# Remainder rows of k and v as tiles of their own, on all 128 partitions

## The chip, the cores and the metric

The kernel runs on one core of one Trainium2 chip, as one launch. The metric is the device time of the launch in microseconds, as the median of several executions. The core has five engines that run side by side and wait for each other by semaphores: TensorE (matrix products), VectorE, ScalarE, GpSimd and SyncE. Sixteen DMA engines move data between the memory in DRAM (HBM) and the core's own memory, SBUF, which has 128 partitions. In the profile the engines are PE (PEld for its weight loads), DVE, ACT, POOL and SP.

## The reference

Two blocks follow each other, all in float32, for 8 batches, 8 heads of 64, and 576 positions. The first is linear attention: for each head a 64 x 64 matrix from k and v, then q by it, then a root-mean-square norm over the 64. The second is an MLP mixer over the positions ("token") and over the 512 channels.

```python
kv = np.einsum('bhsd,bhse->bhde', k, v)
out = np.einsum('bhsd,bhde->bhse', q, kv)
rms = np.sqrt(np.mean(out * out, axis=-1, keepdims=True) + 1e-06)
x = out / rms * g_norm                       # then (B, H, S, D) -> (B, S, H*D)
...
h = np.maximum(x.transpose(0, 2, 1) @ w_tok1, 0.0) @ w_tok2
u = x + h.transpose(0, 2, 1)
return u + np.maximum(u @ w_ch1, 0.0) @ w_ch2
```

The kernel gets k and v as 8 x 576 x 512 (heads beside each other in the last dimension), q transposed as 8 x 512 x 576, and the weights as 64-bit words that it turns into float32 itself ("decoding").

## The kernel before

The change touches the first stage, attention with the token mixing behind it, which fills the first 186 us or so. Batches are taken in four pairs; `side` is the batch within its pair.

The sum over 576 positions doesn't divide by 128: there are four chunks of 128 positions (`J` = 4, `LO` = 512) and a remainder of 64 (`HF` = 64). `k_in[b % 2]` and `v_in[b % 2]` are tiles of 128 partitions x 5 chunks x 512 (`JJ` = 5). `load(b)`, lines 140 to 147, fills each with two DMAs: the main rows (1 MB), and behind it the 64 remainder rows (128 KB) into partitions 0 to 63 of the fifth chunk. Partitions 64 to 127 of that chunk are set to zero once, by the four memsets on GpSimd at line 1285, so that `kv` can treat it as a full chunk. All of these DMAs go through SyncE's queue, v of batch 0 alone through ScalarE's.

`kv(side, half)`, line 371, makes four of the eight 64 x 64 matrices. For each of two pairs of heads `i` and each chunk `j` it issues two products, one for each head `h`, which take one half of the array's columns each:

```python
matmul(o[ds(h * D, D), i, ds(h * D if whole else 0, D)], lhsT=kk[:, j, at],
       rhs=vv[:, j, at],
       start=(j == 0), stop=(j == JJ - 1), skip_group_check=True)
```

Each product is two passes in the trace, so a batch has 80 passes on `ps_kv`. `evict(side, half)` copies the result to SBUF (`kvp`), on VectorE for batch 0 and on ScalarE for the others. `attend` multiplies q by it; `load_q` (main, 1 MB per batch, tile `qT`) and `load_q_rest` (128 KB, `qR`) bring q. The first pair (`whole`) uses full 128 x 128 products with zeros off the diagonal, the later pairs quarters of the array (64 x 64).

The order of all this is written out by hand in lists of short names, `start`, `middle` and `steady` (lines 1297 to 1319), which `play` walks through; every engine keeps that order. `kv01` is the product of side 0, half 1; `e01` its eviction; `l0` the load of the batch that takes side 0 of the next pair; `a`, `g`, `q`, `t` are parts of the attention, `h` and `u` the two products of the token mixing, `f` a fetch of a block of channel weights and the bare numbers decoding steps. Ahead of the lists come the loads of batches 0 and 1 with two blocks of token weights between them, and the third block, `get_tok1_rem` (line 219), which brings the 64 remainder rows of `w_tok1` twice, into the lower and the upper 64 partitions, by two DMAs.

The DMAs issued by SyncE and ScalarE share eight semaphores in rotation. Each issue waits until the DMA eight issues before it has landed, and besides for the tile that it overwrites.

## Time and profile before

| what | us |
|---|---|
| median of 3 runs | 773.67 (773.21 to 774.2) |
| the profiled execution | 772.69 |
| its span, first instruction to last | 770.6 |
| TensorE busy in the span | 760.8 |
| VectorE, ScalarE, GpSimd busy | 642.8, 277.5, 112.3 |
| passes of k by v (`ps_kv`), from the first to the end of the last | 9.2 to 135.7 |

The page gives for each engine the busy time, its share of the span and the number of instructions, and then the span in 40 slices of 19.3 us with the busy share in tenths. The row of DMA is the mean busy share of the sixteen DMA engines. Matrix products are pipelined, so that a full row of PE says that products follow each other without holes, not that each is as fast as it can be. In a line of a timeline the columns are the start, the length, the engine, the source line, the operation, written tile, read tiles, shape, and the number of instructions; an arrow in brackets tells how long the engine was idle before it and who ended that.

### The profile page before, as it was taken

Reading aid. Unit: us, or ns where it says so; the run is one execution under the profiler, and the core shown is the slowest. Engines: PE = TensorE matmul, PEld = TensorE weight load, DVE = VectorE, ACT = ScalarE, POOL = GpSimd, SP = SyncE. Lnnn points to the kernel's source line nnn. Section 1 sums busy time; section 2 is a strip of 40 time slices with the busy share of each in tenths; the row PEclk is TensorE's granted clock in tenths of the full one; section 3 lists DMA queues with packets and bytes.
Section 4 is the critical chain, followed back from the end, with each engine's and each line's share of the span. In section 5 each row is a group of like instructions: output and inputs, shape, how many; then the busy total and the mean of one; then the engine's idle time right before and its main releaser. Section 6 shows DMA issues by size and latency. Waiting matters only on the chain.

```text
span 770.6 us, 12663 instructions
## 1 busy us (share of the span) xinstructions
PE 760.8 (99%) x4682; PEld 612.8 (80%) x4682; DVE 642.8 (83%) x945; ACT 277.5 (36%) x555; POOL 112.3 (15%) x124
## 2 busy tenths in 40 slices
PE   7999999999999999999999999999999999999998
PEld 6665555445888888888888888888888888888887
DVE  2877897997766779999979889987998996798996
ACT  2466575764210233521144242223352224325221
POOL 1002020113410000002240001042000218000204
PEclk9999999999999999999999999999999999999999
DMA  9999999599799786589898577999659879955679
GB/s 308 318 336 385 378 355 358 187 318 338 251 275 355 261 288 194 163 271 203 221 230 257 152 227 220 251 188 271 196 153 284 175 220 205 209 146 155 152 200 119
DMA packets 137819, 188.29 MB, mean 244 GB/s; under 512 B 48800, under 2 KB 95392, under 8 KB 135712
## 3 DMA queue, kind: packets, MB, share of 16 engines
q1 hardware_dynamic: 101744, 167.54, 68.9%
q0 software_dynamic: 34816, 18.36, 15.9%
q10 hardware_dynamic: 1200, 1.61, 0.6%
q8 instruction: 37, 0.61, 0.3%
q14 instruction: 22, 0.18, 0.1%
HBM read 138.31 MB, written 49.15 MB: 243 GB/s over the span
## 4 chain that ended last, share of the span: by engine, by line
PE 97%; DMA 2%; DVE 1%; SPq 0%; issue 0%; ACT 0%
PE ps_d L135 28%; PE ps_b L135 19%; PE ps_a L135 19%; PE ps_h L135 8%; PE ps_u L135 8%; PE ps_v L135 5%; PE ps_c L135 3%; PE ps_o L135 2%; PE ps_kv L135 2%; PE ps_w L135 2%; DMA qT<-in_q_dram 2%; PE ps_r L135 0%; SPq L123 0%; DVE x L451 0%; DVE ms L472 0%; DVE x L509 0%
## 5 line engine op out<-in xcount | busy, mean ns | idle before, releaser
L135 PE MATMUL ps_d<-ui,w 128*128 128x256 f32 x504 | 118.6, 379 | 0.0
L135 PEld LDWEIGHTS ps_d<-ui,w 128*128 128x128 f32 x504 | 95.8, 190 | 13.0
L132 ACT COPY ps_d<-ps_a 128x768 f32<-128x768 f32 (+1 forms) x56 | 32.0, 571 | 199.9 <-PE ps_a L135 196.8
L126 DVE TENSOR_TENSOR v<-v,v 128x1536 f32<-128x1536 f32 (+2 forms) x70 | 103.3, 1483 | 0.3
L135 PE MATMUL ps_b<-sv,w 128*128 128x256 f32 x324 | 78.9, 379 | 0.0
L135 PE MATMUL ps_a<-v,w 128*128 128x256 f32 x324 | 78.7, 379 | 0.0
L1205 POOL DMA_DIRECT2D out_dram<-us x24 | 26.8, 1832 | 291.8 <-ACT p L132 286.2
L135 PEld LDWEIGHTS ps_b<-sv,w 128*128 128x128 f32 x324 | 61.2, 190 | 8.9 <-issue 0.6
L135 PEld LDWEIGHTS ps_a<-v,w 128*128 128x128 f32 x324 | 61.6, 190 | 8.4
L135 PE MATMUL ps_u<-h,w_tok 128*128 128x512 f32 (+1 forms) x160 | 64.7, 599 | 0.0
L135 PE MATMUL ps_d<-v,w 128*128 128x256 f32 x258 | 62.7, 379 | 0.0
L129 ACT ACTIVATE v<-v 128x768 f32<-128x768 f32 (+1 forms) x54 | 42.7, 822 | 55.1 <-DVE v L126 53.5
L135 PE MATMUL ps_h<-x,w_tok 128*128 128x512 f32 x128 | 57.7, 600 | 0.3 <-DVE w_tok L188 0.3
L1205 POOL DMA_DIRECT2D out_dram<-r x40 | 41.3, 1925 | 102.0 <-ACT p L132 80.2
L135 PE MATMUL ps_d<-sv,w 128*128 128x256 f32 x228 | 55.4, 379 | 0.0
L135 PEld LDWEIGHTS ps_d<-v,w 128*128 128x128 f32 x258 | 48.9, 190 | 6.6
L135 PEld LDWEIGHTS ps_u<-h,w_tok 128*128 128x128 f32 (+1 forms) x160 | 25.6, 179 | 31.1 <-issue 26.7
L135 PEld LDWEIGHTS ps_d<-sv,w 128*128 128x128 f32 x228 | 43.3, 190 | 5.9
L135 PE MATMUL ps_a<-uT,w 128*128 128x256 f32 x192 | 46.7, 379 | 0.0
L135 PEld LDWEIGHTS ps_h<-x,w_tok 128*128 128x128 f32 x128 | 23.4, 190 | 27.2 <-issue 24.3
L135 PE MATMUL ps_b<-ui,w 128*128 128x256 f32 x168 | 40.8, 379 | 0.0
L135 PEld LDWEIGHTS ps_a<-uT,w 128*128 128x128 f32 x192 | 36.5, 190 | 5.0
(165 smaller groups left out, 1291.4 us busy)
## 6 DMA issues: line engine op xcount, KB each, us to landing
w<-parts SPq DMA_DIRECT2D x168, 384.0 KB, 3.8
w<-parts SPq DMA_DIRECT2D x56, 192.0 KB, 3.8
uT<-blocks SPq DMA_DIRECT2D x36, 256.0 KB, 5.6
k_in<-in_k_dram SPq DMA_DIRECT2D x8, 1024.0 KB, 13.3
qT<-in_q_dram SPq DMA_DIRECT2D x8, 1024.0 KB, 12.7
out_dram<-x POOLq DMA_DIRECT2D x16, 512.0 KB, 7.5
v_in<-in_v_dram SPq DMA_DIRECT2D x7, 1024.0 KB, 15.8
raw<-in_moe_w_ch_dram SPq DMA_DIRECT2D x8, 768.0 KB, 12.4
```

The costliest lines, as they stand in the source:

```text
L126: keep(engine.tensor_tensor(out=o, in0=a, in1=b, op=op))
L129: keep(nc.scalar.activation(o, a, AF.Relu))
L132: keep(nc.scalar.copy(o, a))
L135: keep(nc.tensor.matmul(*a, **kw))
L1205: keep(nc.gpsimd.dma_start(to, t()[ds(b * Q, Q), at].rearrange("p n l j -> p n (l j)"), accum_op=ALU.add))
```

## The change

The fifth chunk is taken out of `k_in` and `v_in`, and the remainder rows get tiles of their own, `k_rem` and `v_rem`, 128 partitions x 256: heads 0 to 3 of the 64 rows on partitions 0 to 63, heads 4 to 7 on partitions 64 to 127. Each is filled by one DMA whose pattern in DRAM has two halves outermost. `kv` runs over four chunks. A new step, `kv_rest` (`kr0`, `kr1`), makes the remainder's eight products, each of 64 rows by 64 columns, one quarter of the array; it comes after the main products for batch 0 and ahead of them elsewhere, and `start` and `stop` of the accumulation follow that. The remainder loads go ahead of the main ones from batch 1 on. The memsets are gone, and `get_tok1_rem` brings its two copies by one DMA with a zero stride.

```diff
-    k_in = [inp.tile([P, JJ, DM], F32, name=f"k_in{i}") for i in range(2)]
-    v_in = [inp.tile([P, JJ, DM], F32, name=f"v_in{i}") for i in range(2)]
+    k_in, v_in = ([inp.tile([P, J, DM], F32, name=f"{n}_in{i}") for i in range(2)] for n in "kv")
+    k_rem, v_rem = ([inp.tile([P, DH], F32, name=f"{n}_rem{i}") for i in range(2)] for n in "kv")
...
         queues = (nc.sync, nc.sync if b else nc.scalar)
-        for dst, t, e in zip((k_in[b % 2], v_in[b % 2]), (k, v), queues):
-            dma(dst[:, :J], t[b, :LO].rearrange("(p j) e -> p j e", j=J), e)
-            dma(dst[:HF, J], t[b, LO:], e)
+        both = [(k_in[b % 2], k_rem[b % 2], k), (v_in[b % 2], v_rem[b % 2], v)]
+
+        def rest():
+            for (_, dst, t), e in zip(both, queues):
+                r = t[b, LO:, :DH]
+                dma(dst, bass.AP(tensor=r.tensor, offset=r.offset, ap=[[DH, 2]] + list(r.ap)), e)
+
+        if b:
+            rest()
+        for (dst, _, t), e in zip(both, queues):
+            dma(dst, t[b, :LO].rearrange("(p j) e -> p j e", j=J), e)
+        if not b:
+            rest()
...
-        return block(DTOK, lambda raw: [(raw[:HF], w), (raw[HF:], w)], w_tok1r)
+        twice = bass.AP(tensor=w.tensor, offset=w.offset, ap=[[0, 2]] + list(w.ap))
+        return block(DTOK, lambda raw: [(raw, twice)], w_tok1r)
...
+        rest_last = lambda side: whole and side == 0
+
+        def kv_product(side, half, i, h, kk, vv, start, stop):
+            matmul(kv_tile(side, half)[ds(h * D, D), i, ds(h * D if whole else 0, D)], lhsT=kk, rhs=vv,
+                   start=start and i == 0, stop=stop, skip_group_check=True)
+
         def kv(side, half):
...
             for i in range(2):
-                for j in range(JJ):
+                for j in range(J):
                     for h in range(2):
                         at = ds(half * DH + i * P + h * D, D)
-                        matmul(o[ds(h * D, D), i, ds(h * D if whole else 0, D)], lhsT=kk[:, j, at],
-                               rhs=vv[:, j, at],
-                               start=(j == 0), stop=(j == JJ - 1), skip_group_check=True)
+                        kv_product(side, half, i, h, k_in[side][:, j, at], v_in[side][:, j, at],
+                                   j == 0 and rest_last(side), j == J - 1 and not rest_last(side))
+
+        def kv_rest(side):
+            for i in range(2):
+                for half in range(2):
+                    for h in range(2):
+                        r, at = ds(half * HF, HF), ds(i * P + h * D, D)
+                        kv_product(side, half, i, h, k_rem[side][r, at], v_rem[side][r, at],
+                                   not rest_last(side), rest_last(side))
...
-    for t in [t for pair in zip(k_in, v_in) for t in pair]:
-        keep(nc.gpsimd.memset(t[HF:, J], 0.0))
...
-        "j14 kv00 e00", "kv01 e01 l0", "a00 g00 q00", "a01 g01 q01 t00 t01 m0 w01",
+        "j14 kv00 kv01 kr0 e00 e01 l0", "a00 g00 q00", "a01 g01 q01 t00 t01 m0 w01",
...
-        "h000 h010 w12 w13 w14 t10 t11 m1 r1", "h001 h011", "kv10 e10", "kv11 e11 i1 d10 d11 l1", "h002", "a20 q20",
+        "h000 h010 w12 w13 w14 t10 t11 m1 r1", "h001 h011", "kr1 kv10 e10", "kv11 e11 i1 d10 d11 l1", "h002", "a20 q20",
...
-        "h100 h110 h101 h111 w31 w22 w23 w24", "kv00 e00 -lq1 w32 w33 w34",
+        "h100 h110 h101 h111 w31 w22 w23 w24", "kr0 kv00 e00 -lq1 w32 w33 w34",
...
-        "kv10 kv11 e10 e11 t10 t11 m0 r0 lq0", "u3 z6 i0 d00 s01 d11 f1", "u4 l1", "a2 q20 g21 q21 g20",
+        "kr1 kv10 kv11 e10 e11 t10 t11 m0 r0 lq0", "u3 z6 i0 d00 s01 d11 f1", "u4 l1", "a2 q20 g21 q21 g20",
```

The lists of `steady` change in the same way: `kr0` or `kr1` is put ahead of the `kv` of its side.

## The prediction

> **What bounds the kernel now.** I read the page's head first: which engine is full, and whether the DMA engines are.

> ```profile
> span 770.6 us, 12663 instructions
> PE 760.8 (99%) x4682; PEld 612.8 (80%) x4682; DVE 642.8 (83%) x945; ACT 277.5 (36%) x555; POOL 112.3 (15%) x124
> ...
> PE   7999999999999999999999999999999999999998
> ...
> DMA  9999999599799786589898577999659879955679
> ```

> TensorE is full from the second slice to the end, so a lost TensorE microsecond is lost for good; but for the first seven slices (to about 130 us) the 16 DMA engines are full as well. I therefore asked for the page of DMA in the stretch 30 to 130 us, and for the busy time of each engine in stretches (columns: stretch, length, each engine's busy time, clock, DMA share, GB/s).

> ```profile
> DMA packets 14011, 35.72 MB, mean 357 GB/s; under 512 B 4300, under 2 KB 6348, under 8 KB 12566
> ```
> ```profile
> 30.00:60.00 30.00, 30.00 (x371) 17.62 (x370) 22.23 (x50) 17.41 (x47) 0.90 (x1) 1.00 1.04 331
> 60.00:100.00 40.00, 40.00 (x571) 21.73 (x573) 33.38 (x76) 25.09 (x66) 6.73 (x9) 1.00 1.02 370
> 100.00:130.00 30.00, 30.00 (x332) 15.26 (x321) 27.43 (x55) 19.52 (x44) 5.43 (x7) 1.00 1.01 367
> 130.00:160.00 30.00, 30.00 (x367) 15.67 (x367) 23.59 (x48) 19.57 (x51) 6.00 (x8) 1.00 0.69 248
> ```

> So 357 GB/s over 16 engines is 22.3 GB/s for each, 46 ns per KB, with no spare share before 130 us. Last I asked how late the data come, in the timelines of TensorE and ScalarE (start, length, what, then in brackets the idle time before it and who ended it):

> ```profile
> 13.82 2.02 PE L135 MATMUL ps_o<-kvp,qT 128*128 128x128 f32 x16 [1.12 <-DMA qT<-in_q_dram]
> 24.60 2.73 PE L135 MATMUL ps_kv<-v_in,k_in 128*64 128x64 f32 x80
> 83.47 0.93 ACT L164 ACTIVATE w_ch<-raw 128x768 f32<-128x768 f32 x1 [1.81 <-DMA raw<-in_moe_w_ch_dram]
> 126.89 1.23 ACT L173 ACTIVATE w_ch<-raw 128x512 f32<-128x512 f32 x2
> 131.29 0.60 ACT L129 ACTIVATE h<-ps_h 128x512 f32<-128x512 f32 x1 [1.88 <-PE ps_h L135]
> 133.14 2.55 PE L135 MATMUL ps_kv<-v_in,k_in 128*64 128x64 f32 x80
> ```

> The first q lands at 13.7 us and TensorE waited for it. v of batch 1 lands at 24.4 (main) and 25.1 (remainder) against a use at 24.6. Afterwards a margin builds up: v of batch 7 lands 17.9 us after its issue at 101.4, at 119.3, and is used at 133.1. ScalarE waits for a weight block at 83.5. The stream of loads is thus just fast enough, and hardly more.

> [...]

> **The change, part by part.**

> (1) The remainder loads. The new pattern in DRAM is 2 halves x 64 rows x 256 elements, into 128 partitions. Slowest dimensions 2 and 128: k=2. Before, 128 KB went as 64 rows of 2 KB, four rows (8 KB) on each of 16 engines. Now it is 128 rows of 1 KB, 64 on each of engines 0 and 1: 64 KB there, none elsewhere. The trace's packets of 1 KB took 46 ns in the median (mean 58), so one remainder takes 64 x 46 = 2.9 us (3.7), against 4 x 84 ns = 0.34 before. There are 16 of them: +16 x 56 = +896 KB on these two engines.

> (2) `w_tok1r`: its one DMA has 2 (stride zero) x 64 rows outermost: again k=2, 128 KB on each engine instead of 16, +112 KB. One SyncE issue (about 0.5 us) goes away.

> (3) The order of issue. The remainders of batch 1 and later now go ahead of k and v; in batch 0 they stay behind k and v and ahead of q. [...] everything that follows on SyncE's queue (k, v, q, weights) has its share on engines 0 and 1 behind them; a DMA is complete only when its last engine is. Both programs' listings show eight DMA semaphores in rotation: each issue waits for the landing of the eighth before it, so the other 14 engines can't run ahead for long either.

> (4) TensorE. Per batch, 80 half-width passes take 2.55 us (32 ns each). 16 of them become quarters; the quarter passes of `ps_o` take 1.16 us for 64, 18 ns each. Saving 16 x (32-18) = 0.22 us per batch, 1.8 over eight; [...] (bounds -1.8 to +1). If loads bound this stage it is all hidden, since TensorE then waits; I take 0.

> (5) Four POOL memsets (0.52 us each) go: TensorE's first work waits for `ident`, which POOL makes after them, so the warm-up starts 2 us earlier; it then waits for k anyway. Both evictions of batch 0 move behind the remainder products. Memory: the kv tiles shrink by 4 KB per partition in sum. All 0, hidden by the waits for q.

> **Sum for engines 0 and 1.** What one engine has moved before: by the landing of v 7, 8 loads x 144 KB + 7 q x 64 + 6 small q x 8 + token weights 152 + 7 channel blocks x 48 + 8 turned blocks x 8 = 2200 KB, and 256 KB of stores from POOL: 2456 KB from 2.6 us to 119.3, 47.5 ns per KB. For after I take 45 ns: these two engines work partly alone (8 KB packets 321 ns in the median, 40 ns per KB; the 1 KB ones 46). Bounds 42 and 50. Time of landing = 2.6 + 0.045 x KB after:

> - q 0: 64+64+128+64 = 320 KB: 17.0; used at 13.8: 3 us late.
> - v 1: 640 KB: 31.4 against 24.6: 7.
> - v 2: 1104 KB: 52.3 against 39.2: 13.
> - v 4: 1832+32 of stores: 86.5 against 67.9: 19.
> - the weight block used at 86.0, two behind v 5: 2520 KB: 116. ScalarE decodes in order; behind it stands `h` (1.9 us of idle before it), and TensorE has another 1.9 us until it needs `h`: 89.8. 26 late.
> - v 7: 2456-128-16+1024+128 = 3464, +40 of later stores: 160.3 against 133.1: 27.
> - the blocks decoded at 126.9, third of those behind v 7: +16+128+20 = 3668 KB: 167.7. With the same 3.8 us of room (1.88 before 131.29, 1.9 until the product at 135.6), the need is 131.3: 36 late.
> - q 7: +192 KB: 176.3 against 141.0: 35.

> The lateness isn't a sum of stalls: each line says how far the program as a whole is shifted by then; the largest counts, +36. After 130 us the DMA share of 0.69 lets the two engines catch up, and from 186 us TensorE has its operands in time. Queues between: SyncE's waits for a free tile (k 7 waits for the product of k 5) come at TensorE's shifted times, when engines 0 and 1 still have some 20 us queued, so they never run dry. POOL's queue shares the engines, its stores are counted.

> Against the profiled execution: 770.6 + 36 = 807 us of span. That execution took 772.7 (2.1 around the span), the median of runs is 773.7, 1.0 more: 809.5 us forecast.

> **Rivals.**

> *All 16 engines carry the remainders after all* (k taken from the partitions): 128 packets of 1 KB, 8 on each engine, 8 x 46 against 4 x 84 ns, the same. Then (4) counts in the batches from 2 on, where TensorE is full: 6 x 0.22 = 1.3 us: 772.4, between 771.6 and 774.7. This ends at or above the speed of before. The point from which it decides: k=16, or anything at which a remainder costs an engine under about 0.5 us. For it: nothing in this profile shows k below 16. Against it: the pattern as built has the 2 outermost[...].

> *k=2 but paid only at the start*: if the pair of engines were not the slowest afterwards, since the margin of 12 to 14 us at batches 5 to 7 absorbs the rest. The early lines (v 1 to v 4) then give +7 to +15: 781 to 789. Against it: the share of 1.01 to 1.04 until 130 us leaves nothing to catch up with.

> *k=2, slower small packets*: at 50 ns per KB q 7 comes at 195.6, +55: 829. [...] against: half of the time the other 14 engines are idle.

> **How the numbers follow.** Forecast mechanism with 42 to 50 ns per KB (+25 at 42, +55 at 50: 799 to 829) 0.78; paid at the start only 0.09; all 16 engines 0.13. The last splits evenly at -0.2% (772.1 us; about what a measurement of this kernel can tell from no change): faster 0.06, within 0.2% 0.06, slower 0.88. The range, 785 to 830, takes in the first case with both bounds and the upper end of the second.

> **What would show it.** Right: remainders take more than 3 us of two engines, the mean GB/s from 10 to 130 us falls from 357 to about 270, the first q lands near 17 to 19 us, TensorE shows waits for DMA in its first eight slices, its timeline from 190 us on is that of before shifted by about 36, and `ps_kv` has a quarter form (64*64) of 18 ns each. Wrong: TensorE busy from 30 us without holes and DMA still near 357 GB/s means 16 engines. If the shift stops growing before v 5, the margin absorbed it.

## The result and the profile after

The changed kernel takes 806.45 us in the median of 5 runs (805.34 to 807.74), the kernel before 773.21 (772.87 to 774.2): a ratio of 1.0428, 95% interval 1.0413 to 1.0444. It is 33 us slower. The profiled execution took 807.74 us with a span of 806.0.

The head of the page of the changed kernel, with the rows of TensorE, its clock and the DMA engines in 40 slices of 20 us:

```profile
span 806.0 us, 12658 instructions
PE 770.1 (96%) x4682; PEld 618.1 (77%) x4682; DVE 642.0 (80%) x945; ACT 277.0 (34%) x555; POOL 110.4 (14%) x120
...
PE   5969799969999999999999999999999999999998
...
PEclk8989899979999999999999999999999999999999
DMA  6578789887969979658999759889957899955689
```

The holes in TensorE's row lie in the first nine slices; behind them the row is that of before. The DMA engines, which were full up to 130 us, are not full any more in their mean, although the same data have to come. The same stretches as before, columns as before (after the length: busy time of PE, PEld, DVE, ACT, POOL, then clock, DMA share, GB/s):

```profile
10.00:20.00 10.00, 3.56 (x53) 3.26 (x49) 0.76 (x2) 0.00 (x0) 0.00 (x0) 0.65 0.63 191
...
30.00:60.00 30.00, 21.77 (x202) 13.64 (x200) 18.41 (x46) 11.66 (x34) 0.00 (x0) 0.89 0.57 192
60.00:100.00 40.00, 34.84 (x537) 20.49 (x537) 20.92 (x44) 18.39 (x47) 5.67 (x7) 0.91 0.80 277
100.00:130.00 30.00, 29.64 (x361) 15.36 (x359) 21.36 (x48) 15.37 (x39) 1.96 (x4) 1.00 0.90 318
...
160.00:190.00 30.00, 22.51 (x241) 11.14 (x236) 20.54 (x39) 21.77 (x51) 3.58 (x4) 0.83 0.73 253
```

From 30 to 60 us the core moved 192 GB/s at a share of 0.57, where it had moved 331 at 1.04. A mean share of 0.57 with TensorE waiting for data suggests that some engines work and others have nothing to do. A shorter stretch shows how many, first of before, then of after:

```profile
35.00:40.00 5.00, 5.00 (x48) 2.63 (x46) 4.55 (x12) 3.91 (x17) 0.00 (x0) 1.00 1.01 354
```
```profile
35.00:40.00 5.00, 5.00 (x32) 3.76 (x31) 2.54 (x4) 1.19 (x2) 0.00 (x0) 1.00 0.13 50
```

A share of 0.13 is what two engines of sixteen come to (0.125), and 50 GB/s is a little over twice the 22.3 that one engine moved before. TensorE's timeline tells how late the data were (lines left out are marked):

```profile
17.93 6.41 PE L135 MATMUL ps_o<-kvp,qT 128*128 128x128 f32 x32 [1.70 <-DMA qT<-in_q_dram]
...
32.49 2.09 PE L135 MATMUL ps_kv<-v_in,k_in 128*64 128x64 f32 x64 [1.61 <-DMA v_in<-in_v_dram]
...
53.52 1.98 PE L135 MATMUL ps_kv<-v_in,k_in 128*64 128x64 f32 x32 [4.94 <-DMA v_in<-in_v_dram]
...
88.98 3.68 PE L135 MATMUL ps_kv<-v_in,k_in 128*64 128x64 f32 x64 [5.16 <-DMA v_in<-in_v_dram]
...
117.90 5.42 PE L135 MATMUL ps_u<-h,w_tok 128*128 128x512 f32 x12
...
159.05 2.08 PE L135 MATMUL ps_kv<-v_in,k_in 128*64 128x64 f32 x64
168.62 7.82 PE L135 MATMUL ps_u<-h,w_tok 128*128 128x512 f32 x12 [7.49 <-ACT h L129]
176.37 1.16 PE L135 MATMUL ps_o<-kvp,qT 64*64 64x64 f32 x64
```

All but the one at 159.05 are compared with the kernel before, where they stood at 13.82, 24.60, 39.18, 67.92, 93.93, 135.62 and 140.97 us; three of these lines are

```profile
39.18 1.39 PE L135 MATMUL ps_kv<-v_in,k_in 128*64 128x64 f32 x40
...
67.92 2.55 PE L135 MATMUL ps_kv<-v_in,k_in 128*64 128x64 f32 x80
...
135.62 5.42 PE L135 MATMUL ps_u<-h,w_tok 128*128 128x512 f32 x12
```

The shift grows as 4.1, 7.9, 14.3, 21.1, 24.0, 33.0 and 35.4 us (in the second to fourth, 0.4 us of it is the quarter products that now stand ahead), and from there it is kept: the span is 35.4 us longer. The last stall is put down to `h` on ScalarE, whose own timeline shows what stood ahead of it:

```profile
161.19 0.89 ACT L174 ACTIVATE w_ch<-raw 128x768 f32<-128x768 f32 x1 [6.88 <-DMA raw<-in_moe_w_ch_dram]
...
165.16 1.21 ACT L183 ACTIVATE w_ch<-raw 128x512 f32<-128x512 f32 x2 [2.29 <-DMA raw<-in_moe_w_ch_dram]
...
167.50 2.04 ACT L129 ACTIVATE h<-ps_h 128x512 f32<-128x512 f32 x4
```

ScalarE keeps the order of the lists: it waits 6.88 and 2.29 us for weight blocks that lie in SyncE's queue behind v of batch 7, decodes them, and only then, at 167.50 us, makes `h`. TensorE's product of k by v for batch 7, the line at 159.05, had not waited at all.

**How many engines carried a remainder** can also be read from the page's packet counts. The queue lines give packets, MB and share; here those of before, then of after:

```profile
q1 hardware_dynamic: 101744, 167.54, 68.9%
...
q10 hardware_dynamic: 1200, 1.61, 0.6%
```
```profile
q1 hardware_dynamic: 102464, 167.54, 66.1%
...
q10 hardware_dynamic: 1250, 1.61, 0.6%
```

q10 is ScalarE's queue. It has one remainder in it, v of batch 0: 64 packets of 2 KB became 128 of 1 KB, +64, but the count rose by 50. Fourteen are missing. The traces hold, beside the data, small packets of 4 B: before, 112 of them in q10, 16 for each of its seven DMAs, and 8112 in q1, 16 for each of 507. After, q10 has 98. That fits one such packet on every engine that a DMA uses; this one left 2 instead of 16. In q1, 15 remainders: +15 x 64 - 15 x 14 = +750, and the token block (two DMAs on 16 engines become one on 2, -30): +720, which is the difference to the packet. k, the number of engines that carry a DMA, was 2.

The landing marks in the changed kernel's trace agree, two at the landing of each remainder (a third comes behind its issue) and sixteen at that of a main load, and they tell what TensorE waited for. Of the sixteen of the first q, fourteen come from 11.7 to 13.6 us and two at 17.6 and 17.8, and TensorE starts at 17.93; of v of batch 1, fourteen from 28.0 to 28.7 and two at 32.2 and 32.4, and TensorE starts at 32.49. The last marks of batch 1's loads come in the order of issue: the remainders of k and v at 23.7 and 27.5 us, k at 29.8, v at 32.4, q at 34.9.

### The profile page after: what moved, and what is told of

It is laid out like the page before. It is cut to its first block, busy times and chain, and to the rows that moved or that the text cites. A ratio compares the mean times of both kernels' runs of the same rounds, so it can differ in the third digit from the quotient of the medians.

```text
span 806.0 us, 12658 instructions
## 1 busy us (share of the span) xinstructions
PE 770.1 (96%) x4682; PEld 618.1 (77%) x4682; DVE 642.0 (80%) x945; ACT 277.0 (34%) x555; POOL 110.4 (14%) x120
## 4 chain that ended last, share of the span: by engine, by line
PE 79%; DMA 1%; ACT 0%; DVE 0%; SPq 0%; issue 0%; ACTq 0%
PE ps_d L135 27%; PE ps_b L135 18%; PE ps_a L135 18%; PE ps_v L135 5%; PE ps_u L135 4%; PE ps_c L135 3%; PE ps_h L135 2%; PE ps_w L135 2%; DMA raw<-in_moe_w_ch_dram 1%; PE ps_o L135 0%; ACT w_ch L183 0%; ACT raw L186 0%; ACT h L129 0%; PE ps_r L135 0%; DVE xs L126 0%; SPq L123 0%
## 5 line engine op out<-in xcount | busy, mean ns | idle before, releaser
L135 PE MATMUL ps_d<-ui,w 128*128 128x256 f32 x504 | 118.6, 379 | 0.0
L135 PEld LDWEIGHTS ps_d<-ui,w 128*128 128x128 f32 x504 | 95.8, 190 | 13.0
L135 PE MATMUL ps_b<-sv,w 128*128 128x256 f32 x324 | 78.9, 379 | 0.0
L135 PE MATMUL ps_a<-v,w 128*128 128x256 f32 x324 | 78.7, 379 | 0.0
L135 PE MATMUL ps_u<-h,w_tok 128*128 128x512 f32 (+1 forms) x160 | 68.6, 633 | 8.4 <-ACT h L129 7.5
L135 PEld LDWEIGHTS ps_b<-sv,w 128*128 128x128 f32 x324 | 61.2, 190 | 8.9 <-issue 0.5
L135 PEld LDWEIGHTS ps_a<-v,w 128*128 128x128 f32 x324 | 61.6, 190 | 8.4
L135 PE MATMUL ps_d<-v,w 128*128 128x256 f32 x258 | 62.7, 379 | 0.0
L129 ACT ACTIVATE v<-v 128x768 f32<-128x768 f32 (+1 forms) x54 | 42.6, 822 | 55.1 <-DVE v L126 55.1
L135 PE MATMUL ps_h<-x,w_tok 128*128 128x512 f32 x128 | 58.9, 609 | 0.5 <-ACT x L529 0.3
L135 PEld LDWEIGHTS ps_u<-h,w_tok 128*128 128x128 f32 (+1 forms) x160 | 26.9, 190 | 42.1 <-issue 27.8
L135 PE MATMUL ps_d<-sv,w 128*128 128x256 f32 x228 | 55.4, 379 | 0.0
L135 PEld LDWEIGHTS ps_d<-v,w 128*128 128x128 f32 x258 | 48.9, 190 | 6.6
L135 PEld LDWEIGHTS ps_d<-sv,w 128*128 128x128 f32 x228 | 43.3, 190 | 5.9
L135 PE MATMUL ps_a<-uT,w 128*128 128x256 f32 x192 | 46.7, 379 | 0.0
L475 DVE TENSOR_TENSOR x<-ps_o,g_sb 128x512 f32<-128x512 f32 x32 | 21.3, 685 | 31.8 <-ACT sq L479 19.4
L135 PEld LDWEIGHTS ps_h<-x,w_tok 128*128 128x128 f32 x128 | 23.8, 193 | 28.4 <-issue 23.9
L123 POOL DMA_DIRECT2D out_dram<-x x24 | 16.4, 684 | 181.2 <-DVE x L126 151.0
```

Source lines behind the costliest of these rows:

```text
L123: keep(engine.dma_start(o, i))
L129: keep(nc.scalar.activation(o, a, AF.Relu))
L135: keep(nc.tensor.matmul(*a, **kw))
L475: keep(nc.vector.tensor_mul(x, bank[c, h], g_sb.to_broadcast([P, number(c), D])))
```

## The experiments

All times are medians; each ratio is to runs of the kernel before on the same chip.

**1. The changed kernel, two DMAs per remainder.**

```diff
-                r = t[b, LO:, :DH]
-                dma(dst, bass.AP(tensor=r.tensor, offset=r.offset, ap=[[DH, 2]] + list(r.ap)), e)
+                for i in range(2):
+                    dma(dst[ds(i * HF, HF)], t[b, LO:, ts(i, DH)], e)
...
-        return block(DTOK, lambda raw: [(raw, twice)], w_tok1r)
+        return block(DTOK, lambda raw: [(raw[:HF], w), (raw[HF:], w)], w_tok1r)
```

> The changed kernel, but each remainder is loaded by two DMAs of 64 rows, one per half of the partitions, and the third token block by two again: same tiles, order, quarter products and 1 KB packets, and 64 rows outermost, so 16 engines carry each. Theory (two engines carry 64 KB of each remainder and everything queues behind it): the whole loss goes, and 1.3 us of TensorE's gain are left, 772 us (771 to 774.5). Rival (the loss comes from the new order of the loads, from the smaller packets or from the quarter products): 800 us or more.

Measured: 772.16 us against 773.29, ratio 0.9987 (0.9981 to 0.9993). The whole loss is gone, with the same tiles, order, packet size and quarter products. What is left of the change is a gain of 0.13%, about 1 us, at the limit of what can be told. Its stretches have no hole from 30 us on:

```profile
30.00:60.00 30.00, 30.00 (x373) 17.51 (x372) 22.41 (x50) 17.51 (x47) 0.90 (x1) 1.00 1.03 366
60.00:100.00 40.00, 40.00 (x604) 21.71 (x606) 33.28 (x75) 25.34 (x67) 6.73 (x9) 1.00 1.04 381
```

The quarter products are seen in TensorE's timeline of this kernel, undisturbed by waits:

```profile
67.72 0.46 PE L135 MATMUL ps_kv<-v_rem,k_rem 64*64 64x64 f32 x16
68.11 2.08 PE L135 MATMUL ps_kv<-v_in,k_in 128*64 128x64 f32 x64
70.03 1.89 PE L135 MATMUL ps_u<-h,w_tok 128*64 128x512 f32 x8
```

From start to start the 16 quarter passes take 0.39 us (24 ns each, not the 18 of a long run of quarters in `ps_o`), the 64 others 1.92: 2.31 in all, where before it was 67.92 to 70.31, 2.39. The saving per batch is about 0.1 us and not 0.22.

**2. The token block alone put back.** As in the second half of the diff above.

> The changed kernel, but the third token block comes by two DMAs as before; the remainders of k and v stay as changed. Theory: 112 KB less on the two engines from batch 2 on, at 45 ns per KB 5 us less: 801.4 us (799 to 804). Rival (this block is off the path, it is needed late): 806.5. Rival (this block is most of the loss): below 790.

Measured: 803.23 us, ratio 1.0381 (1.0365 to 1.0397): 3.2 us less than the changed kernel. The block has its part, the remainders the rest. The size was expected at 5.

**3. The kernel before, with k=2 and nothing else.**

```diff
-            dma(dst[:HF, J], t[b, LO:], e)
+            r = t[b, LO:]
+            dma(dst[:HF, J], bass.AP(tensor=r.tensor, offset=r.offset, ap=[[DM, 2], [2 * DM, HF // 2], [1, DM]]), e)
```

> The kernel before, untouched but for the pattern in DRAM of the remainder loads: even rows, then odd rows (2 x 32 rows of 2 KB, the same for k and v, so the sums don't change), 2 outermost. No quarter products, no new order, no token block by one DMA, packets of 2 KB as before. Theory: the pair of engines gets the same 896 KB more as in the changed kernel, at 42 ns per KB for packets of 2 KB; less the token block: +28, 801 us (795 to 804). Rival (order, packet size or products are the cause): 773 to 775.

Measured: 803.86 us, ratio 1.0390 (1.0373 to 1.0406). Not a byte, tile, packet size or product of the kernel before differs, only the order of the 64 rows, and nearly the whole loss is there. This run and run 1 together leave no other part of the change as the main cause.

**4. The order of the loads put back.** In the changed kernel:

```diff
-        if b:
-            rest()
...
-        if not b:
-            rest()
+        rest()
```

> The changed kernel with the remainders of every batch behind the main rows of k and v in the queue, as in the kernel before. Theory: the bytes ahead of a batch's last operand on the two engines are the same, so nothing but a microsecond or two moves: 806.5 us (803 to 809). Rival (it is the new order that makes k and v late): below 790.

Measured: 804.91 us, ratio 1.0403 (1.0384 to 1.0422), an interval that overlaps that of the changed kernel (1.0413 to 1.0444). The ratios put the order at about 2 us, which the intervals don't tell from nothing; most of the loss isn't there.

**5 and 6. Four and eight engines,** in the kernel before. The same edit as in 3, with 4 and 8 in place of 2.

> The kernel before with the remainder rows in an order of 4 x 16, 4 outermost: 32 KB of each remainder on four engines instead of 8 KB on sixteen. Theory: 16 x 24 = 384 KB more on the slowest engine, 17 us of its time by the end of the loads, less the room that there was (1.2 us at v of batch 2, 4.7 at the weight blocks behind v of batch 7): the blocks come 8 us late at 45 ns per KB: 781 us (778 to 786). Rival (the loss is a property of exactly two engines, or of any pattern with three dimensions): 773 or about 801.

> The kernel before with the remainder rows in an order of 8 x 8, 8 outermost: 16 KB on eight engines. Theory: 128 KB or 5.8 us more by the end, which the room of 4.7 us nearly swallows; 0.7 us late at the first q, 1.4 at v of batch 1: 775 us (773 to 778). Rival (a three-dimensional pattern costs by itself): above 780.

Measured: 783.9 us with four, ratio 1.0138 (1.0120 to 1.0155); 773.4 with eight, ratio 0.9999 (0.9989 to 1.0009). The first queue's packet counts confirm k; from above, the pages of the kernels with k of 2, 4 and 8:

```profile
q1 hardware_dynamic: 101534, 167.54, 67.5%
```
```profile
q1 hardware_dynamic: 101564, 167.54, 67.8%
```
```profile
q1 hardware_dynamic: 101624, 167.54, 68.5%
```

These are 101744 less 15 x 14, 15 x 12 and 15 x 8. The pattern with three dimensions costs nothing by itself (0.9999 with eight outermost), and the loss grows with what the slowest engine carries beyond its share: 128, 384 and 896 KB in sum give 0, 10.5 and 30.6 us. Per KB that is nothing, 27 and 34 ns, nearing the 45 ns per KB that the prediction took, its estimate for no room left. The 1.5 us expected for eight engines were not there.

**7. The token block alone,** in the kernel before: one DMA of zero stride.

> The kernel before, with the third token block alone by one DMA of zero stride, 2 outermost. Theory: 112 KB more on two engines, 5 us at v of batch 2, whose room is 1.2 us: 3.8 us late, 777 us (775 to 779). By the run without it in the changed kernel, which was 3.2 us faster, perhaps 776. Rival (the block is needed only at 40.7 us, so it costs nothing): 773.

Measured: 777.2 us, ratio 1.0048 (1.0031 to 1.0065): 3.8 us, the sum that was expected. The block itself doesn't hold TensorE; what it delays is v of batch 2 behind it:

```profile
41.93 2.16 PE L135 MATMUL ps_kv<-v_in,k_in 128*64 128x64 f32 x40 [2.62 <-DMA v_in<-in_v_dram]
```

But the sum isn't made as expected. This product is 2.75 us later than at 39.18 before, not 3.8, and it then takes 2.16 us instead of 1.39 and the next group 4.50 instead of 3.70, at half the clock: the mean is 0.57 from 42 to 46 us. That adds 1.6 us, 4.3 in all in this trace, so that the size agrees partly by luck.

**8 and 9. The pair of engines in part of the batches only.** Run 1 with one DMA per remainder for batches 6 and 7, and for batches 0 and 1:

```diff
+                if b >= 6:
+                    r = t[b, LO:, :DH]
+                    dma(dst, bass.AP(tensor=r.tensor, offset=r.offset, ap=[[DH, 2]] + list(r.ap)), e)
+                else:
+                    for i in range(2):
+                        dma(dst[ds(i * HF, HF)], t[b, LO:, ts(i, DH)], e)
```

(in the second, `b < 2`.)

> The changed kernel with two DMAs per remainder and for the token block (772.2 us), but with the one DMA of 2 halves for the remainders of batches 6 and 7 alone. Theory: 4 x 56 = 224 KB, 10 us at 45 ns per KB, for all that stands behind v of batch 7; k and v of batches 6 and 7 have 13.8 us of room and aren't waited for, but the weight blocks decoded at 127 us have 4.7 in all: 5.4 us late, 777.5 us (775 to 781). Rival (only the wait of k by v counts, and its room absorbs it): 772.

> The changed kernel with two DMAs per remainder and for the token block (772.2 us), but with the one DMA of 2 halves for the remainders of batches 0 and 1 alone. Theory: the first q comes 4 us and v of batch 1 8 us late, as in the changed kernel; that is never given back, since TensorE is full from there on, but nothing is added either, as the later loads have their room again: 780.7 us (779 to 783). This is what the rival that pays only at the start would have come to. If later lateness came from the first batches' backlog too: above 785.

Batches 0 and 1 alone: 780.42 us, ratio 1.0088 (1.0074 to 1.0101), as expected; the start is worth 8 of the 33 us. Batches 6 and 7 alone: 774.05 us, ratio 1.0007 (0.9998 to 1.0015), 1.9 us more than run 1 and not 5.4. The way was the expected one, and the size was wrong. Timelines of ScalarE and TensorE, first of run 1, then of this one:

```profile
126.37 1.26 ACT L183 ACTIVATE w_ch<-raw 128x512 f32<-128x512 f32 x2
130.72 0.60 ACT L129 ACTIVATE h<-ps_h 128x512 f32<-128x512 f32 x1 [1.80 <-PE ps_h L135]
...
134.83 5.42 PE L135 MATMUL ps_u<-h,w_tok 128*128 128x512 f32 x12
```
```profile
132.23 1.28 ACT L187 ACTIVATE w_ch<-raw 128x512 f32<-128x512 f32 x2 [0.89 <-DMA raw<-in_moe_w_ch_dram]
...
134.69 2.04 ACT L129 ACTIVATE h<-ps_h 128x512 f32<-128x512 f32 x4
...
135.81 5.42 PE L135 MATMUL ps_u<-h,w_tok 128*128 128x512 f32 x12 [1.13 <-ACT h L129]
```

The wait of ScalarE for the blocks, and TensorE's for `h`, are new, and k by v waits for nothing: the chain is right. But the decoding moved by 5.9 us and TensorE by 1.0; a second wait for `h`, 0.77 us at 171.25, makes up most of the rest of the 1.9. The product begins before the four tiles of `h` are all made (they take from 134.69 to 136.73), so the room behind the decoding is larger than the 3.8 us that were taken, 4.9 by these lines, and in run 1 the blocks land about 2 us earlier than in the kernel before (by 124.8 us against 126.6).

**10. A longer warm-up.** Run 1 with 19 warm-up products for 14.

```diff
-        "j14 kv00 kv01 kr0 e00 e01 l0", ...
+        "j19 kv00 kv01 kr0 e00 e01 l0", ...
```

> The changed kernel with two DMAs per remainder and for the token block, and with 19 warm-up products in place of 14. Without the memsets the warm-up ends 2 us earlier, TensorE then sits idle for 2.4 us until v lands and runs the first products of k by v at half the clock (64 passes in 3.6 us instead of 2.1). Theory: with the longer warm-up those run at full clock, and the wait for the eviction of 0.5 us before the first product with q gives way to that for q, 0.2 us earlier: 771.9 us, not to be told from 772.2. Rival (the slow start costs more than that): 771 or less.

Measured: 772.10 us, ratio 0.9984 (0.9975 to 0.9993): not to be told from run 1. The first products of k by v run at full clock again (64 passes in 2.08 us, where run 1 took 3.59), and the first product with q starts at 13.80 us, after a wait for q, where in run 1 it started at 14.01, after a wait of 0.5 us for the eviction. But the half clock isn't gone, it comes later (a mean of 0.83 from 10 to 20 us). So a slow start costs no more than some tenths of a microsecond here; what half the clock costs by itself this run doesn't show, and its trace is of the slowest of its eleven executions.

Of the ten, runs 1 and 10 are the only ones whose interval lies below 1, by 0.13 to 0.16%. That is less than the 0.2% that the prediction took as the limit of what can be told, so no gain should be built on it.

## Why the prediction was right

The forecast was 809.5 us, between 785 and 830; measured 806.45.

*Step (1) and (2), k=2.* Right, and shown directly by the packet counts, by the share of 0.13 where two engines alone work, and by runs 1, 3, 5 and 6. The trace of before had no such case: that a dimension of 2 outermost puts a DMA on two engines was the author's assumption. The packet counts bear it out for this case's patterns, with 2, 4 and 8 outermost on 2, 4 and 8 engines and 64 rows on 16. Which two of the sixteen they are (the prediction says 0 and 1) isn't told by any record here.

*The sum for the two engines.* Line by line, lateness forecast and measured: first q 3 and 4.1; v of batch 1, 7 and 7.9; v of batch 2, 13 and 14.3; v of batch 4, 19 and 21.1; v of batch 7, 27, not waited for, as TensorE itself was 25.6 us late there by then; the blocks behind it 36, of which 33.0 reached TensorE. The weight block of 86 us, forecast at 26, never held TensorE: ScalarE decoded it at 115.1 us without a wait, and `h` was made in time. The 24.0 us at `ps_u` (117.90) are the 21.1 of v of batch 4, 2.3 that half clock right behind it added (the 64 passes at 88.98 took 3.68 us and not 2.08, the next eight of `ps_u` 3.18 and not 1.89; the quarters, already done, give back 0.5), and 0.6 that came at the following product of k by v. The slope of 45 ns per KB was a little low at first (v of batch 4: 88.98 less 2.6 over 1864 KB, 46.3) and a little high at the end (third block, decoded on arrival at 165.16: over 3668 KB, 44.3). That the stall ends with weight blocks that hold up ScalarE, and not with k or v, came out as forecast. The size of that line did not quite: the third block was there at 165.2 us and not at 167.7, and TensorE's product followed the start of its decoding by 3.5 us where before it was 8.7, a room of 5.3 us and not 3.8. The need of 131.3 us isn't 126.9 and 3.8 either; that is 130.7, with which the line would have read 37.0. Less 2.5 for the landing and 1.5 for the room, that gives the 33.0.

*The mean rate.* 270 GB/s from 10 to 130 us was forecast, the stretches give 261.

*What the sum lacked: the clock.* In the changed kernel TensorE's granted clock was at half in four stretches (about 13.1 to 23.3, 50.6 to 57.4, 88.2 to 95.0 and 163.3 to 173.5 us; a mean of 0.65 in 10 to 20 us and of 0.83 in 160 to 190 us), each of which began within one of its four longest waits in this stage (4.75, 4.94, 5.16 and 7.49 us). After the last stall the 12 passes of `ps_u` took 7.82 us instead of 5.42; these 2.4 us lie on the path and lead from 33.0 to 35.4. The 2.3 us of half clock behind v of batch 4 hardly add to the end, as the last wait, 7.49 us, is longer. Two errors met: the landing and the room of the blocks were mis-sized, by some 3 us too much, and the clock wasn't priced. So it is in part luck that the 36 comes so near to 35.4. What brings on the half clock stays open: in these traces it comes with a wait, but a wait of 2.62 us was followed by it in run 7 and one of 2.56 us was not in run 3 (a clock of 1.00 from 53 to 57 us).

*Step (4), the quarters.* The saving was taken as hidden, and in the changed kernel it is. Its size was wrong: 0.1 us per batch for 0.22. A group of 16 quarter passes between groups of other shapes takes 24 ns a pass and not 18, and the passes that they replace take 30 ns from start to start and not 32. What makes a pass of the short group dearer isn't shown by any run.

*Step (5), at nothing.* Nearly: without the memsets the warm-up ends earlier, and in run 1 the first products run slowly after the gap and the first product with q starts 0.2 us later than before (14.01 against 13.82). In the changed kernel itself v of batch 0 came earlier, and it was the remainder and q that were waited for.

*The rivals.* All sixteen engines would have given 772.4 us; run 1, which brings it about, took 772.16. Paid at the start only would have been 781 to 789; run 9 gives 780.42, just below. (The lower bound of the first, 771.6, isn't 773.7 less 1.8, which is 771.9.)

## What to carry to other kernels

Before a DMA is given a new pattern, look at the outermost dimension of both its sides, as built: here a dimension of 2, for "two halves at once" or "twice by zero stride", put the whole transfer on two of sixteen engines (2 small packets for 16). Two DMAs of 64 rows each cost one more issue and used all sixteen (run 1: q10 has 1280 packets, 80 more than before, which are 64 of data and 16 small ones). And where, as here up to 130 us, the mean share of the DMA engines was near 1 (1.01 to 1.04), the price of such a transfer wasn't its own latency, but its excess on the slowest engine, for everything that was queued behind it, less the room there (runs 3 and 5: 34 and 27 ns per KB): sum that engine's KB up to each operand and compare with when it is used.
